# Attention and a multiplicative feed-forward on one core: the first two score groups of each batch change places, and the order of all work is recomputed

## The chip, the cores and the metric

The kernel runs on one core of a Trainium2 chip. The core has TensorE (PE, matrix products), ScalarE (ACT), VectorE (DVE), GpSimd (POOL) and SyncE (SP). DMAs are issued by POOL, SP and, once, ACT. The metric is the time of one execution on the device in microseconds (us); of several runs the median is taken.

## The reference

There are 8 batches and 8 heads, 576 queries and keys of 64 numbers per head, and 16 beacon keys and values per head, which every query sees. The other keys are causal.

```python
k_all = np.concatenate([beacon_k, k], axis=2)          # 16 + 576 keys
v_all = np.concatenate([beacon_v, v], axis=2)
scores = scale * np.matmul(q, k_all.transpose(0, 1, 3, 2))
causal[:, Nb:] = np.triu(np.ones((S, S), dtype=bool), k=1)
scores = np.where(causal, -1e9, scores)
a = np.exp(scores - scores.max(-1, keepdims=True))
a /= a.sum(-1, keepdims=True) + 1e-09
attn = np.matmul(a, v_all)                             # then x = tokens x (heads * 64)
a = x @ w1; b = x @ w2
h = a * b @ w3
return (h @ w_out).astype(np.float32)                  # 4608 x 512
```

w1 and w2 are 512 x 1024, w3 is 1024 x 1024 and w_out 1024 x 512.

## The kernel before

The program is one long list, ORDER, of small steps separated by semicolons. It was computed ahead of time. A step is a name with numbers: `s 0 1 2` is the function s with batch 0, group 1, bank 2. The loop at the end calls them one after the other, and each engine runs its own instructions in exactly this order. An instruction waits until the data that it reads is there and the place that it writes is free; everything behind it on its engine waits with it.

**Loads.** lq, lk and lv load chunks of queries, keys and values (128 tokens, all heads; of batch 0 a chunk number of lq and lk is a pair of heads instead), lkb and lvb the beacon keys and values, l1 and l2 quarters of w1 and w2, l3 eighths of w3, lo quarters of w_out. All but the first two (S and A) are issued by POOL, which also issues most stores (st); at most eight of its DMAs are under way in the trace at a time.

**Queries and keys.** In batch 0, cast turns a pair of heads into 16-bit numbers (ACT or DVE), tq or tk transposes it on TensorE, eq or ek copies it out. In batch 1 and for part of batch 2 there is no cast. Other chunks are transposed by a DMA that SP issues (Dq, Dk). tn and en do the same for the beacon keys of batch 0.

**Scores.** A batch is four pairs of heads (t) with 13 groups of blocks. A group fills 512 columns of each head's scores. make_groups lists them: for each t a corner group (the blocks with the first 112 queries, which see the beacon, and those with the last 80), and runs of four 128 x 128 blocks that NINE lists. s computes a group in two banks, exp evicts it on ACT to one of eight ring slots (line 517), m masks the diagonal blocks (DVE, line 527), v multiplies by the values (line 538), n divides by the sums (DVE, lines 549 and 550).

**Between.** x (TensorE, line 564) and ex, or TX (a DMA of SP), transpose the result to xT.

**Feed-forward.** W = w3 @ w_out is formed once: t3 transposes an eighth of w3, e3 copies it out, f multiplies by w_out (line 492), ew copies the result out. For each of nine blocks of 512 tokens (mc), a and b are the products with w1 and w2 (line 579), ea scales and copies a (ACT or DVE, lines 299 and 301), eb multiplies it by b (DVE, line 594), o multiplies by W (line 600), eo copies out, st stores.

**Banks.** The last number of a step on TensorE is its bank: 0 is a pair for scores, 6 and 7 are single ones, 2 with 3 and 4 with 5 are used as a pair or as two. A step waits until the copy that reads its bank's last content is done.

**Spins.** spin multiplies zeros, to keep TensorE at work before there is data.

Of the kernel before, what the change touches and what calls it, by code (L numbers as in the profile page):

```python
# [696 lines left out]
```

## Time and profile before

| | us |
|---|---|
| median of 4 runs (291.25 to 292.49) | 291.94 |
| the profiled execution's own time | 292.93 |
| its span, first to last instruction | 291.2 |
| TensorE busy | 283.9 |
| DVE, ACT, POOL busy | 171.7, 147.3, 134.3 |

The profile is of one execution. A busy share in it is an average over a head in which data arrives, a long middle and an end. A TensorE step's duration overlaps the next one's; the time from one start to the next is what it costs. The clock granted to TensorE has a mean of 0.998.

### The profile page before, as it was taken

How to read it: one execution, taken by the hardware profiler on the slowest of the kernel's cores; microseconds unless marked ns; L12 is line 12 of the kernel's file. 1: busy time of each engine (PE TensorE's matmuls, PEld its weight loads, DVE VectorE, ACT ScalarE, POOL GpSimd, SP SyncE). 2: the span in 40 equal slices, each digit the busy share in tenths (PEclk: the TensorE clock that was granted, in tenths of full speed). 3: DMA queues.
4: the chain of work that ended last, by engine and by line, in shares of the span. 5: the costliest groups of instructions: out<-in, count | busy, mean ns of one | idle time of the engine just before them, and what ended most of it. 6: DMA issues, size and time to landing. Idle time of an engine off the chain costs nothing.

```text
span 291.2 us, 7032 instructions
## 1 busy us (share of the span) xinstructions
PE 283.9 (97%) x2904; PEld 153.9 (53%) x2904; DVE 171.7 (59%) x370; ACT 147.3 (51%) x188; POOL 134.3 (46%) x187
## 2 busy tenths in 40 slices
PE   7999999999999999999999999999999999999993
PEld 3536675565565555565544555555555445444442
DVE  4344587885686847565562666565755575677600
ACT  3767779636574655588126567547482162000031
POOL 8869888797569551384098554630010011000000
PEclk9999999999999999999999999999999999999999
DMA  9999999999999999699999999996220015100043
GB/s 163 199 200 174 172 174 177 170 154 140 162 203 144 131 157 211 114 130 169 150 137 129 202 205 155 150 193 140 47 92 2 36 66 143 55 2 0 23 157 110
DMA packets 154319, 38.87 MB, mean 133 GB/s; under 512 B 144112, under 2 KB 150000, under 8 KB 154288
## 3 DMA queue, kind: packets, MB, share of 16 engines
q0 software_dynamic: 114800, 26.46, 107.1%
q1 hardware_dynamic: 39280, 11.68, 26.7%
q8 instruction: 23, 0.38, 0.5%
q10 hardware_dynamic: 208, 0.29, 0.4%
q14 instruction: 8, 0.07, 0.1%
HBM read 39.32 MB, written 9.44 MB: 167 GB/s over the span
## 4 chain that ended last, share of the span: by engine, by line
PE 75%; DMA 14%; POOL 8%; issue 1%; ACT 0%; POOLq 0%; SPq 0%
PE one L579 38%; PE one L600 21%; PE one L538 8%; PE pair L507 7%; DMA w<-in_moe_w_dram 5%; DMA st<-in_k_dram 2%; DMA qT<-q 2%; POOL va L339 2%; DMA wo<-in_moe_w_out_dram 2%; POOL q L331 2%; DMA q<-in_q_dram 2%; POOL k L339 1%; POOL w L389 1%; POOL xT L398 1%; PE one L564 0%
## 5 line engine op out<-in xcount | busy, mean ns | idle before, releaser
L579 PE MATMUL one<-xT,w 128*128 128x512 f16 x576 | 133.6, 379 | 0.0
L517 ACT ACTIVATE ring<-pair 128x1024 f16<-128x1024 f32 x104 | 99.2, 1027 | 21.4 <-PE pair L507 19.4
L579 PEld LDWEIGHTS <-w 128*128 128x128 f16 x576 | 52.9, 98 | 59.4 <-issue 2.5
L600 PE MATMUL one<-Wt,gT 128*128 128x512 f16 (+1 forms) x296 | 66.5, 374 | 0.0
L594 DVE TENSOR_TENSOR gT<-one,asb 128x512 f16<-128x512 f32 x72 | 49.1, 689 | 23.2 <-PE one L579 16.3
L299 ACT ACTIVATE asb<-one 128x512 f32<-128x512 f32 x32 | 19.2, 600 | 75.4 <-PE one L579 49.4
L614 POOL DMA_DIRECT2D out_dram<-st x27 | 15.3, 569 | 63.3 <-DVE st L301 29.5
L600 PEld LDWEIGHTS <-gT 128*128 128x128 f16 x296 | 27.7, 98 | 30.7 <-issue 1.3
L339 POOL DMA_DIRECT2D va<-in_v_dram x40 | 34.0, 853 | 20.7 <-PE one L538 15.4
L538 PEld LDWEIGHTS <-ring 128*128 128x128 f16 x960 | 35.2, 97 | 9.9 <-issue 1.0
L538 PE MATMUL one<-va,ring 128*128 128x65 f16 x960 | 37.6, 193 | 0.0
L301 DVE TENSOR_SCALAR asb<-one 128x512 f32<-128x512 f32 x40 | 27.5, 689 | 14.8 <-PE one L579 14.0
L339 POOL DMA_DIRECT2D k<-in_k_dram x35 | 29.8, 857 | 13.3 <-DMA kT<-k 9.4
L331 POOL DMA_DIRECT2D q<-in_q_dram x35 | 30.0, 863 | 7.7 <-DMA va<-in_v_dram 2.6
L550 DVE TENSOR_TENSOR x<-one,rd 128x384 f16<-128x384 f32 (+1 forms) x64 | 31.4, 491 | 2.2
L507 PE MATMUL pair<-qT,kT 64*128 64x80 f16 (+4 forms) x736 | 30.8, 225 | 0.1
L507 PEld LDWEIGHTS <-kT 64*128 64x128 f16 x736 | 19.8, 95 | 14.7 <-issue 11.9
L299 ACT ACTIVATE st<-one 128x512 f32<-128x512 f32 (+1 forms) x18 | 10.3, 574 | 24.3 <-PE one L600 24.0
L527 DVE TENSOR_TENSOR ring<-ring,MD 128x768 f16<-128x768 f16 x32 | 17.7, 552 | 7.9 <-ACT ring L517 7.9
L301 DVE TENSOR_SCALAR st<-one 128x512 f32<-128x512 f32 x19 | 13.1, 690 | 14.1 <-PE one L600 14.1
L527 DVE TENSOR_TENSOR ring<-ring,MX 128x384 f16<-128x384 f16 x32 | 11.3, 354 | 16.4 <-ACT ring L517 16.4
L549 DVE RECIPROCAL rd<-one 128x6 f32<-128x6 f32 (+1 forms) x64 | 11.7, 183 | 12.2 <-PE one L538 11.9
(63 smaller groups left out, 134.8 us busy)
## 6 DMA issues: line engine op xcount, KB each, us to landing
out_dram<-st POOLq DMA_DIRECT2D x27, 256.0 KB, 7.3
q<-in_q_dram POOLq DMA_DIRECT2D x28, 128.0 KB, 6.8
va<-in_v_dram POOLq DMA_DIRECT2D x24, 128.0 KB, 7.4
k<-in_k_dram POOLq DMA_DIRECT2D x21, 128.0 KB, 7.1
xT<-in_moe_w_dram POOLq DMA_DIRECT2D x8, 256.0 KB, 6.2
w<-in_moe_w_dram POOLq DMA_DIRECT2D x8, 256.0 KB, 7.3
out_dram<-st SPq DMA_DIRECT2D x8, 256.0 KB, 2.0
wo<-in_moe_w_out_dram POOLq DMA_DIRECT2D x4, 256.0 KB, 6.2
```

Source lines behind the costliest of these rows:

```text
L299: nc.scalar.activation(dst, src, AF.Copy, scale=by)
L301: nc.vector.tensor_scalar(dst, src, by, None, ALU.mult)
L331: nc.gpsimd.dma_start(dst[:rows, c], src[b, :, ds(c * P, rows), :].rearrange("h s d -> s h d"))
L339: nc.gpsimd.dma_start(dst[ds(p0, rows), c], src[b, :, ds(s0, rows), :].rearrange("h s d -> s h d"))
L507: nc.tensor.matmul(shape(n, "pair")[:, hh, ds(col, w)], kT[ds(hh * 64, 64), t, ts(jt, P)], qT[ds(hh * 64, 64), t, ds(q0, w)],)
L517: nc.scalar.activation(held(b, g)[:, :, 0:GW], shape(n, "pair"), AF.Exp, scale=scale)
L527: nc.vector.tensor_tensor(blk, blk, msk, ALU.mult)
L538: nc.tensor.matmul(pv[:, 2 * at + hh, 0 : D + 1], held(b, g)[:, hh, ds(col, P)], va[:, jt, 2 * t + hh, 0 : D + 1], start=(jt == 0), stop=( ...
L550: nc.vector.tensor_tensor(x16s[b % NB2][:, ds(2 * h, ni), ts(t, P)].rearrange("p i (h d) -> p i h d", h=2), pv[:, 0 : 2 * ni, 0:D].rearran ...
L579: nc.tensor.matmul(bank(n), w12[:, kt, ds(i * DF + kf * P, P)], xT[:, kt, ds(mc * 512, 512)], start=(kt == 0), stop=(kt == NKT - 1),)
L594: nc.vector.tensor_tensor(gTs[mc % 2][:, kf, :], bank(n), asb[slot["asb", (mc, kf)]], ALU.mult)
L600: nc.tensor.matmul(bank(n)[:, 0:w], gTs[mc % 2][:, kf, ts(mt, P)], Wt[:, kf, ds(c0, w)], start=(kf == 0), stop=(kf == NFT - 1),)
```

## The change

make_groups appends the corner group of the first pair of heads behind the first run instead of ahead of it. So group 0 of each batch now holds the blocks of keys 1, 3, 2 and 2 (in chunks of 128) with queries 112 to 495, none of which reads chunk 0, where the beacon keys lie; group 1 is the corner. Other groups keep their numbers. All of ORDER is new: the sequence of steps, their banks, which engine copies, which chunks of x go by TensorE and which by DMA, and the order of the loads. The steps are the same ones but for these choices, one spin entry less (20 spins become 17) and the split of the last o, eo and st (256 and 256 columns become 384 and 128).

```diff
     for t in range(4):
         corner = [(t, 0, 0, 0, 112), (t, 4, 4, 112, 80)]
         corner += [(t, j, 4, 192 + 80 * j, 80) for j in range(4)]
-        groups.append(corner)
+        if t:
+            groups.append(corner)
         for jt, i in NINE[t]:
             run.append((t, jt, i, 128 * len(run), 128))
             if len(run) == 4:
                 groups.append(run)
                 run = []
+                if len(groups) == 1:
+                    groups.append(corner)
```

The head of ORDER up to the first scores of batch 1, the places where batch 2 begins, and the end:

```diff
-consts 0; lq 0 0 S; lk 0 0 A; l3 6; consts 1; spin 8 7; lq 1 2 P; l3 4; lo 1; lkb 0 P;
-cast 0 0 q A; lo 0; cast 0 0 k D; lkb 1; consts 2; spin 2 7; tq 0 0 6; tk 0 0 7; eq 0 0 D 6;
-lq 0 1 P; ek 0 0 A 7; spin 1 0; t3 6 5; lk 0 1 P; e3 6 A 5; spin 1 6; tq 1 2 6; l3 3; eq 1 2 A 6;
-spin 3 7; t3 4 7; lvb 0; e3 4 D 7; lo 2; spin 3 6; tn 0 6; en 0 A 6; lk 1 0 P; spin 1 7; s 0 0 0;
-s 0 1 2; s 0 2 4; exp 0 0 0; f 6 0 7; l3 0; f 4 0 6; lk 0 2 P; exp 0 2 4; m 0 0 0; f 6 1 7;
-cast 0 1 q D; lo 3; f 4 1 6; cast 0 1 k D; exp 0 1 2; tq 0 1 5; lk 0 3 P; tk 0 1 4; ek 0 1 D 4;
-eq 0 1 A 5; spin 1 0; t3 3 3; lq 0 3 P; m 0 0 1; l3 5; s 0 3 0; s 0 4 4; e3 3 D 3; exp 0 3 0;
-f 6 2 7; lvb 1; f 3 0 3; exp 0 4 4; m 0 1 0; l3 2; s 0 5 0; tk 1 0 2; f 3 1 3; exp 0 5 0; t3 0 5;
-lq 0 2 P; f 3 2 3; e3 0 D 5; ek 1 0 A 2; lk 1 1 P; f 4 2 6; cast 0 2 k A; m 0 1 1; f 0 0 4;
-f 0 1 4; lv 0 4; f 0 2 4; f 6 3 7; cast 0 3 k A; l3 1; f 0 3 4; ew 6 D 7; lv 0 0; tk 0 3 5;
-ew 0 A 4; f 4 3 6; cast 0 3 q D; ek 0 3 A 5; tq 0 3 7; ew 4 D 6; t3 5 4; lv 1 0; eq 0 3 A 7;
-f 3 3 3; e3 5 D 4; lv 0 2; tk 0 2 6; ew 3 A 3; t3 2 7; ek 0 2 A 6; lv 0 3; f 5 0 5; e3 2 D 7;
-f 5 1 5; cast 0 2 q A; lv 0 1; f 5 2 5; f 5 3 5; lq 1 3 P; tq 0 2 6; ew 5 D 5; tk 1 1 7;
-eq 0 2 A 6; f 2 0 4; l1 2; ek 1 1 D 7; s 0 6 0; s 0 7 2; l3 7; exp 0 6 0; t3 1 6; lq 1 1 P;
-f 2 1 4; e3 1 D 6; f 2 2 4; exp 0 7 2; lq 1 4 P; f 2 3 4; m 0 2 0; lq 1 0 P; f 1 0 7; ew 2 A 4;
-f 1 1 7; lk 1 2 P; f 1 2 7; f 1 3 7; lk 1 3 P; v 0 1 0 6; ew 1 A 7; v 0 2 0 5; n 0 1 0 6; tq 1 3 4;
-lk 1 4 P; v 0 0 0 7; n 0 2 0 5; eq 1 3 A 4; s 0 8 0; n 0 0 0 7; v 0 0 1 6; exp 0 8 0; lv 1 3;
-s 0 9 2; s 0 10 4; s 0 11 0; n 0 0 1 6; exp 0 9 2; l1 0; t3 7 7; m 0 2 1; v 0 1 1 6; e3 7 D 7;
-exp 0 11 0; lv 1 1; tq 1 1 3; tq 1 4 2; n 0 1 1 6; f 7 0 7; eq 1 4 A 2; l2 0; f 7 1 7; exp 0 10 4;
-m 0 3 0; s 0 12 0; m 0 3 1; lq 2 1 P; v 0 3 0 6; eq 1 1 D 3; tk 1 2 2; exp 0 12 0; v 0 2 1 5; l1 1;
-n 0 3 0 6; f 7 2 7; n 0 2 1 5; ek 1 2 A 2; lv 1 2; x 0 4 6; x 0 0 4; v 0 3 1 3; ex 0 4 A 6;
-ex 0 0 D 4; l2 1; f 7 3 7; n 0 3 1 3; tq 1 0 6; lv 1 4; tk 1 4 5; tk 1 3 4; eq 1 0 D 6; ek 1 4 A 5;
-x 0 2 3; x 0 3 2; lq 2 0 P; ek 1 3 D 4; ex 0 2 A 3; x 0 1 6; ex 0 3 D 2; s 1 0 0; s 1 1 4; s 1 2 2;
...
-Dk 2 3; v 1 3 0 3; exp 1 12 4; ea 0 5 D 7; b 0 6 2; lq 3 2 P; ek 2 4 D 6; m 1 3 1; b 0 4 6; lv 2 2;
-n 1 3 0 3; v 1 3 1 7; eb 0 6 2; x 1 4 5; x 1 0 4; n 1 3 1 7; lq 3 4 P; tk 2 1 3; b 0 5 2;
-ek 2 1 A 3; ex 1 0 D 4; lk 3 2 P; ex 1 4 D 5; v 1 2 1 7; eb 0 5 2; Dq 2 4; tq 2 2 5; lk 3 1 P;
-b 0 7 4; n 1 2 1 7; eq 2 2 A 5; lk 3 4 P; a 0 4 5; eb 0 7 4; lvb 2; Dq 3 1; x 1 1 7; ea 0 4 A 5;
-lq 3 3 P; x 1 3 4; ex 1 1 D 7; x 1 2 3; tq 2 3 2; ex 1 3 A 4; eb 0 4 6; o 0 2 7; ex 1 2 A 3;
-lk 4 3 P; eq 2 3 D 2; Dq 3 2; lq 3 0 P; eo 0 2 D 7; s 2 0 0; s 2 1 4; s 2 2 2; exp 2 0 0; lk 4 0 P;
...
-o 7 3 7; eo 7 2 D 6; st 7 2 S; o 7 0 6; eo 7 3 A 7; st 7 3 S; o 8 3 7; eo 7 0 A 6; st 7 0 S;
-o 7 1 6; eo 8 3 A 7; st 8 3 S; o 8 2 7; eo 7 1 A 6; st 7 1 S; o 8 0 6 0 256; eo 8 2 A 7; st 8 2 S;
-eo 8 0 A 6 0 256; st 8 0 S 0 256; o 8 0 5 256 256; eo 8 0 A 5 256 256; st 8 0 S 256 256
+consts 0; lq 0 0 S; lk 0 0 A; l3 5; consts 1; spin 8 7; lkb 0 P; lk 0 2 P; lq 0 1 P; l3 2; lo 0;
+cast 0 0 q D; l3 0; consts 2; cast 0 0 k D; spin 1 7; tq 0 0 6; lv 0 2; eq 0 0 D 6; tk 0 0 7;
+ek 0 0 A 7; spin 1 0; t3 5 5; l3 3; s 0 0 0; lk 0 1 P; e3 5 D 5; tn 0 6; cast 0 2 k A; lo 1;
+en 0 D 6; spin 2 7; s 0 1 2; s 0 2 4; cast 0 1 q A; lk 1 1 P; tk 0 2 6; exp 0 2 4; tq 0 1 7; lo 3;
+eq 0 1 D 7; ek 0 2 A 6; t3 2 5; f 5 0 7; lo 2; exp 0 1 2; e3 2 D 5; spin 1 6; f 2 0 6; exp 0 0 0;
+m 0 0 0; lv 0 1; t3 0 5; lkb 1; e3 0 A 5; m 0 0 1; f 0 0 4; l3 4; t3 3 5; cast 0 1 k A; lq 0 2 P;
+e3 3 D 5; spin 3 0; tk 0 1 3; f 3 0 5; lq 1 2 P; ek 0 1 D 3; f 5 1 7; f 3 1 5; lv 0 3; spin 1 3;
+tk 1 1 3; f 2 1 6; ek 1 1 A 3; f 0 1 4; l3 6; s 0 3 0; s 0 4 2; exp 0 3 0; f 3 2 5; lk 1 0 P;
+f 3 3 5; exp 0 4 2; m 0 1 0; lv 0 4; s 0 5 0; ew 3 D 5; f 0 2 4; l3 1; exp 0 5 0; f 0 3 4; f 5 2 7;
+lvb 0; ew 0 A 4; t3 4 5; m 0 1 1; lv 0 0; f 5 3 7; cast 0 2 q A; e3 4 D 5; f 2 2 6; lq 0 3 P;
+tq 1 2 4; ew 5 D 7; f 4 0 5; f 4 1 5; eq 1 2 D 4; lk 0 3 P; f 4 2 5; f 4 3 5; t3 6 7; l2 1;
+ew 4 A 5; tq 0 2 4; e3 6 D 7; tk 1 0 3; lk 1 2 P; eq 0 2 A 4; f 2 3 6; ek 1 0 D 3; ew 2 A 6;
+s 0 6 0; s 0 7 4; l3 7; f 6 0 7; exp 0 6 0; lkb 2; t3 1 6; f 6 1 7; lv 1 0; exp 0 7 4; m 0 2 0;
+v 0 0 1 3; lk 1 4 P; cast 0 3 q D; s 0 8 0; e3 1 A 6; n 0 0 1 3; lq 1 1 P; tq 0 3 5; v 0 1 0 4;
+v 0 2 0 2; eq 0 3 D 5; exp 0 8 0; lq 1 3 P; v 0 0 0 6; n 0 2 0 2; f 1 0 3; lv 1 2; cast 0 3 k A;
+f 1 1 3; n 0 0 0 6; f 1 2 3; lq 1 0 P; n 0 1 0 4; tk 1 2 6; tk 0 3 5; ek 1 2 A 6; f 6 2 7; m 0 2 1;
+f 6 3 7; ek 0 3 A 5; lvb 1; lq 1 4 P; ew 6 D 7; s 0 9 0; s 0 10 4; l1 3; exp 0 9 0; t3 7 6;
+tk 1 4 7; lk 1 3 P; v 0 1 1 2; e3 7 D 6; exp 0 10 4; f 1 3 3; m 0 3 0; l1 0; tq 1 1 6; ek 1 4 D 7;
+ew 1 A 3; s 0 11 0; s 0 12 4; n 0 1 1 2; l1 2; tq 1 3 7; exp 0 11 0; v 0 3 0 3; eq 1 1 D 6; l2 0;
+v 0 2 1 2; eq 1 3 D 7; exp 0 12 4; m 0 3 1; tq 1 0 6; lv 1 3; f 7 0 7; eq 1 0 D 6; f 7 1 7;
+lq 2 0 P; n 0 2 1 2; tq 1 4 6; v 0 3 1 5; eq 1 4 A 6; n 0 3 0 3; f 7 2 7; l1 1; f 7 3 7; n 0 3 1 5;
+lq 2 2 P; x 0 0 6; ew 7 A 7; x 0 4 4; tk 1 3 3; ex 0 0 D 6; x 0 3 5; lv 1 4; ex 0 4 A 4;
+ek 1 3 D 3; x 0 1 7; x 0 2 6; ex 0 3 A 5; ex 0 1 D 7; lv 1 1; s 1 0 0; s 1 1 2; s 1 2 4;
...
+tq 2 0 5; ea 0 3 D 7; a 0 2 6; lq 2 3 P; eq 2 0 A 5; m 1 1 1; v 1 1 0 7; lv 2 0; v 1 0 1 4;
+ea 0 2 A 6; n 1 1 0 7; tq 2 2 5; b 0 3 6; n 1 0 1 4; lvb 2; eq 2 2 A 5; v 1 0 0 7; lk 2 4 P;
+eb 0 3 6; s 1 6 0; s 1 7 2; s 1 8 4; Dk 2 0; n 1 0 0 7; exp 1 6 0; a 0 7 6; lq 2 1 P; exp 1 8 4;
+m 1 2 0; b 0 4 7; lk 2 3 P; exp 1 7 2; m 1 2 1; tk 2 2 5; lv 2 4; v 1 2 0 4; ek 2 2 D 5; lkb 3;
+s 1 9 0; s 1 10 2; Dq 2 4; n 1 2 0 4; exp 1 9 0; v 1 1 1 5; lq 3 2 P; eb 0 4 7; a 0 6 4;
+exp 1 10 2; m 1 3 0; ea 0 7 D 6; tq 2 3 7; lv 2 1; s 1 11 0; s 1 12 2; ea 0 6 A 4; eq 2 3 D 7;
+v 1 3 0 6; lk 3 0 P; n 1 1 1 5; Dq 3 4; exp 1 11 0; v 1 2 1 7; n 1 3 0 6; tk 2 4 4; lkb 4; a 0 5 5;
+exp 1 12 2; lk 2 1 P; ek 2 4 D 4; m 1 3 1; x 1 0 6; x 1 4 4; tq 2 1 3; lv 2 2; ex 1 0 D 6;
+ex 1 4 A 4; v 1 3 1 2; eq 2 1 D 3; Dk 2 3; b 0 6 6; n 1 2 1 7; lv 2 3; b 0 2 4; n 1 3 1 2;
+lq 4 1 P; eb 0 6 6; x 1 2 7; lq 3 0 P; x 1 1 3; Dq 3 2; ex 1 2 A 7; x 1 3 2; eb 0 2 4; b 0 7 6;
+lk 3 2 P; ex 1 3 A 2; ex 1 1 D 3; b 0 5 7; ea 0 5 D 5; lv 3 0; Dk 3 0; eb 0 7 6; b 1 2 4; lk 3 3 P;
+eb 0 5 7; o 0 3 6; lk 3 1 P; a 1 2 7; lk 4 4 P; eo 0 3 D 6; tk 2 1 5; ea 1 2 D 7; a 1 3 6;
+ek 2 1 A 5; lk 3 4 P; eb 1 2 4; s 2 0 0; s 2 1 2; s 2 2 4; ea 1 3 A 6; exp 2 1 2; b 1 0 7; lvb 3;
...
+a 7 5 4; eb 8 6 6; o 8 1 7; eb 7 3 5; ea 7 5 D 4; eb 7 5 3; o 7 3 6; eo 8 1 D 7; st 8 1 S; o 7 1 7;
+eo 7 3 A 6; st 7 3 S; o 8 0 6; eo 7 1 A 7; st 7 1 S; o 7 2 7; eo 8 0 D 6; st 8 0 S; o 8 3 6;
+eo 7 2 A 7; st 7 2 S; o 7 0 7; eo 8 3 A 6; st 8 3 S; o 8 2 6 0 384; eo 7 0 D 7; st 7 0 S;
+eo 8 2 A 6 0 384; st 8 2 S 0 384; o 8 2 5 384 128; eo 8 2 D 5 384 128; st 8 2 S 384 128
```

## The prediction

> **What bounds the kernel now.** I read the page's first two parts, then TensorE by stretches, its waits, the chain, and last the loads one by one.
>
> ```profile
> PE 283.9 (97%) x2904; PEld 153.9 (53%) x2904; DVE 171.7 (59%) x370; ACT 147.3 (51%) x188; POOL 134.3 (46%) x187
> PE   7999999999999999999999999999999999999993
> POOL 8869888797569551384098554630010011000000
> DMA  9999999999999999699999999996220015100043
> ```
>
> TensorE is busy for 97% of the span; ACT and DVE have room. POOL, which issues the loads, and the DMA engines are full for the first third. By stretches:
>
> ```profile
> 0.00:20.00 20.00, 18.12 (x155) 9.06 (x156) 8.51 (x25) 11.83 (x15) 15.10 (x31) 1.00 1.15 185
> 20.00:40.00 20.00, 19.20 (x274) 12.37 (x273) 11.57 (x28) 14.70 (x21) 18.59 (x24) 1.00 1.94 175
> 40.00:60.00 20.00, 20.00 (x288) 12.12 (x285) 15.66 (x37) 15.76 (x20) 16.36 (x22) 1.00 2.03 174
> 60.00:80.00 20.00, 19.93 (x238) 11.42 (x237) 12.91 (x31) 10.32 (x14) 15.50 (x20) 1.00 2.24 151
> 80.00:240.00 160.00, 160.00 (x1704) 86.60 (x1703) 99.18 (x215) 87.36 (x108) 67.71 (x91) 1.00 1.46 134
> ```
>
> Columns: stretch, its length, then the busy time of PE, weight loads, DVE, ACT, POOL; clock, DMA share, GB/s. TensorE loses time before 40 us and none from 80 to 240. So the order decides two things: how late TensorE runs behind its loads in the head, and whether some later transfer misses it. The chain says the same:
>
> ```profile
> 47.33 7.94 DMA w<-in_moe_w_dram
> 55.55 0.86 POOL q L331
> 56.41 5.17 DMA q<-in_q_dram
> 61.65 6.99 DMA qT<-q
> 68.69 0.79 PE pair L507 x20
> ...
> 245.23 27.63 PE one L579 x128
> 272.86 13.85 PE one L600 x72
> ```
>
> Up to 68.69 us the end is traced back through loads, behind it through TensorE alone. Two rows give the price of TensorE's steps:
>
> ```profile
> 160.66 0.86 PE one L579 x4
> 161.53 0.77 PE pair L507 x22
> 162.30 0.97 PE one L579 x4
> ```
>
> Four products of L579 take 0.86 us, and 0.97 beside scores: going from a score matmul (64 rows) to another kind, or back, costs 0.10. From start to start I read per step: a, b 0.862; o 1.726; f 0.431; v 0.367 and 0.543; a score group 0.224; t3 0.458; a transposed chunk 0.22 to 0.26; a spin 0.215, each of the first eight 0.423.
>
> **The change part by part.** *The swap itself.* All score groups, products and score matmuls (736) remain. Of 104 groups 63 follow another group directly in both orders, so there are 82 changes of kind at 0.10 in both: nothing. In batch 0 the first group can start before the beacon's transpose: its scores move from 10.64 us to about 7.2, but nothing behind them starts earlier than its own load.
>
> *Spins.* 20 become 17: 3 x 0.215 = 0.6 us less TensorE work. It is a gain only if TensorE isn't waiting for a load there instead.
>
> *Evictions and transposes.* ACT and DVE swap a few copies (ea 32 to 31 on ACT, eq 8 to 4); 17 x steps and 23 TX remain, three of each changing places. Covered by engines at 51% and 59%; uncovered, one is 0.6 to 1.0 us. SP has 76 transposes before and after; their order changes, its first comes earlier (below).
>
> *The loads' order, the term that counts.* Landing times are issue plus time to landing, by tile. In the head POOL's loads land one behind the other, at intervals that depend on the kind: 256 KB of weights 1.25 us, a batch-0 pair of heads 0.73, a 128 KB chunk 0.87, 112 KB 0.76, 80 KB 0.52, 64 KB 0.45, a beacon 0.2. From the first landing at 6.26 these intervals give l3 0 at 17.53 (17.47 in the trace). Then one load (lk 0 2, issued 12.08) lands at 19.33 instead of 18.2, and all later ones run 0.6 to 0.9 late.
>
> The last load that stops TensorE for certain in the old head is lq 1 4, landing at 36.56, the 35th on POOL; its transposes start at 36.61. Summing the steps behind that point: 241.6 + 70 changes x 0.097 = 248.4. The trace has its last matmul done at 286.69, that is 250.1: 1.65 of small rests, which I carry over.
>
> In the new order the corresponding load is lq 1 0, the 38th. Ahead of it stand the same loads but for: lv 1 2 (0.87), lk 1 2 (0.87), lk 1 4 (0.52) and lq 1 0 in place of lq 1 4 (0.42): 36.56 + 2.68 = 39.24. The start adds some: the old stream began with two weights and a chunk in its first three loads, a backlog; the new one has the beacon and two pairs behind one weight, and none of the head's loads landed sooner than 4.8 us after its issue. By that bound the third and fourth (issued about 2.9 and 3.5) land at 7.7 and 8.3 instead of 7.2 and 7.9: 0.4 to 0.7. So lq 1 0 lands at 39.6 to 39.9; I take 39.75. Behind tq 1 0 stand 240.1 + 66 x 0.097 = 246.5 us of TensorE work. End of TensorE: 39.75 + 0.05 + 246.5 + 1.65 = 288.0, against 286.7: **+1.3**.
>
> As a check from the other side, what TensorE waits for on its way. tq 0 1 waits for lq 0 1 (8.3 to 8.6) and its cast, now on ACT (0.83 instead of 0.36 to 0.41 on DVE): 0.5. t3 2 waits for bank 5, pair 4 being read by an exp (1.02): 0.65. f 0 0 follows t3 0 at once and waits for e3 0, now on ACT behind two exps (1.01 instead of 0.69): 1.3; behind it on TensorE stands t3 3, whose weights land at 14.1 to 14.5 anyway. tk 0 1 waits for another cast on ACT: 0.5. tk 1 1 waits for lk 1 1: 0.4. f 3 2 needs lo 2, now the last of its four (about 20.5; the old order had lo 2 at 15.45 and lo 3 at 20.26): 0.8. With 0.7 ahead of the first transpose and some 1.6 of smaller ones: 6.5, against 4.9 in the same reckoning of the old order. 1.7 less 0.6 of spins is +1.1. I take +1.2.
>
> *Later stages.* Scores of batches 2 to 7 start by TensorE's own sum 2.0, 0.9, 1.5, 5.0, 0.1 and 14.7 us later than before, besides the lag; their last key or query load stands 3.2, 1.0, 3.0, 2.8, 1.9 and 5.1 us of intervals later. Slack of the old trace covers most (Dk 3 3 lands at 90.2 for scores at 92; the last of batch 4 at 114.9 for 118). Two places have almost none: lv 1 1 for v 1 1 (about 52) and lk 2 1 for s 2 0 (about 72.3). I add 0.1, with bounds 0 and 1.5.
>
> *End.* The last piece is 128 columns wide, not 256: its copy is at most the 0.38 of the old one, its transfer at most the old 3.2. I take -0.1; bounds -0.4 and 0.
>
> Sum: 1.2 + 0.1 - 0.1 = +1.2. The span goes from 291.2 to 292.4; the profiled execution's own time of 292.93 (1.7 around the span) becomes 294.1. It lay 1.0 above the median of four runs, 291.94, to which the same +1.2 gives **293.1**.
>
> **One rule against the rows.** The clock. In the trace the first eight spins take 0.423 and later ones 0.215: TensorE comes up at half rate. The new head has fewer spins and a longest wait of 1.3 us. If the clock fell back once, and took as long to return, 8 x 0.208 = +1.7 us would be lost.
> The Trainium skill, "TensorE: Matmul & The Clock Gate" (Part 1), has the clock fall only after an idle window of about 3.4 us; by it, estimated, 1.3 us of waiting costs no clock and the sum stays at +1.2. No run yet shows such a gap.
>
> **The rivals.**
> *Not slower: the stream keeps its intervals.* The lag at lk 0 2 belongs to one moment, not to every order. Without it lq 1 0 lands at 38.9 or sooner, and f 3 2 waits 0.1 instead of 0.8: about +0.3, 292.2. For it: l3 0 and everything ahead of it land within 0.1 of the intervals. Against: most loads up to 50 us stay late. It decides if lq 1 0 lands before 38.9. If the start bound falls too (0.5) and TensorE has only the old head's 4.3 us of waits, its work allows 33.7 + 4.3 = 38.0 at tq 1 0: -0.5 or, with some evictions earlier, 290.8; that is the faster side.
> *Slower by more: batch 2 misses its keys.* SP's first transpose goes out at about 54 instead of 57.25, and four, not three, go out ahead of lk 2 1. In the old trace loads fell behind their intervals by 1.1 us after three transposes and 2.3 after four. lk 2 1, at 66.9 by intervals, lands at 69.3 and is transposed on TensorE at 71.1. It decides if the four cost over 4 us: then s 2 0 and all behind it wait, +1.5 on top, 294.6.
> *The clock falls back once:* 294.8, as above.
>
> **How the numbers follow.** Forecast 0.50 (own range 292.4 to 293.9; 0.12 of it under 292.8); stream undisturbed 0.25 (0.20 within, 0.05 below); batch 2 late 0.15; clock 0.05; faster through earlier evictions 0.05. A measurement here can tell about 0.3%, 0.9 us. Faster 0.05 + 0.05 = 0.10; within 0.20 + 0.12 = 0.32; slower 0.38 + 0.15 + 0.05 = 0.58. Range: 291.3 (the 38.0 above) to 295.2 (both slow rivals' part, or a later miss).
>
> **What would show it.** Right: TensorE busy for under 18 us in the first 20; f 0 0 and f 3 2 starting about 1 us late; tq 1 0 at 39.8; no idle time from 80 to 240; 17 spins. Wrong: tq 1 0 before 38.9, matmuls of 0.42 after 10 us, or a wait at s 2 0. What I may have wrong above all is the landing intervals in a new order.

## The result, and the profile after

The changed kernel takes 292.68 us (median of 54 runs, 291.34 to 296.45). The kernel before, run beside it, takes 292.04 us (78 runs, 291.18 to 294.21). The ratio is 1.0022 with a 95% interval of 1.0013 to 1.0031: slower, by 0.64 us. (One of the 54 executions, that of 296.45 us, was in a slower state and is left out of the ratio.) That is inside the range on record (291.3 to 295.2) and has the sign that was forecast, but it is half of the +1.2 us, and by the bound of 0.3% it counts as "within", which had been given a chance of 0.32 against 0.58 for "slower".

The profiled execution of the changed kernel has a span of 290.7 us and an own time of 292.38 us. The span of the one before was 291.2 us, although its kernel is the faster one. The reason lies behind TensorE's last matmul. In the old execution 4.5 us followed it, because its last store took 3.2 us to land; in other executions with the same end, shown below, that store lands in 1.7 us and about 3.1 us follow. In the changed one 3.1 us follow. So the two are compared by TensorE's end: 286.69 us before, 287.56 us after, +0.87.

The page of the changed kernel, its first two parts:

```profile
PE 283.2 (97%) x2901; PEld 154.2 (53%) x2901; DVE 171.7 (59%) x372; ACT 146.7 (50%) x186; POOL 134.7 (46%) x187
...
PE   6989999999999999999999999999999999999995
...
POOL 8868996999537783402985400577020001000000
...
DMA  7999999999999999995999991499983012300033
```

As before, TensorE is busy for 97%, and the only slices that are not full lie in the head and at the end. By stretches (stretch, length, busy time of PE, weight loads, DVE, ACT, POOL; clock, DMA share, GB/s):

```profile
0.00:20.00 20.00, 15.94 (x125) 8.23 (x125) 8.74 (x24) 9.03 (x11) 15.35 (x29) 1.00 1.17 180
20.00:40.00 20.00, 19.83 (x294) 12.80 (x293) 12.12 (x30) 15.60 (x21) 17.83 (x26) 1.00 1.85 177
40.00:60.00 20.00, 19.86 (x270) 11.94 (x270) 14.42 (x35) 14.56 (x20) 16.94 (x23) 1.00 2.09 167
60.00:80.00 20.00, 20.00 (x213) 11.19 (x213) 14.01 (x32) 10.57 (x16) 16.44 (x21) 1.00 2.40 166
80.00:240.00 160.00, 160.00 (x1724) 87.08 (x1723) 99.00 (x213) 86.84 (x107) 67.08 (x90) 1.00 1.39 135
```

TensorE was busy for 18.12 us of the first 20 before and is busy for 15.94 now; from 20 to 40 us it gains 0.63, from 40 to 60 it loses 0.14. From 60 to 240 us it never stops. So whatever the change costs is decided before 60 us. The chain of work that ended last, up to 55 us and its two longest pieces at the end (start, length, what):

```profile
11.20 9.16 DMA wo<-in_moe_w_out_dram
...
22.50 6.28 DMA xT<-in_moe_w_dram
...
41.70 8.32 DMA w<-in_moe_w_dram
50.06 1.04 PE one L583 x4
...
246.96 26.76 PE one L583 x124
273.72 13.85 PE one L604 x72
```

Before, the chain ran through loads up to 68.69 us. Now the last load on it is l1 1, a quarter of w1, which lands at 50.02 us (41.70 + 8.32), and from 50.06 TensorE alone sets the end. The loads ahead of it are lo 2 (landing at 20.37) and l3 1 (28.78), one behind the other in POOL's queue: none of them is a load of queries.

To see how much TensorE waited, I took the distance from each of its steps to the next and subtracted the step's own length from the prediction (and 0.10 for a change between scores and other work). What is left, summed in us:

| start of the step | 0 to 20 | 20 to 40 | 40 to 60 | 60 to 100 | behind 100 | sum |
|---|---|---|---|---|---|---|
| before | 2.49 | 1.81 | 0.32 | 0.43 | 0.69 | 5.74 |
| after | 5.55 | 0.31 | 0.63 | 0.12 | 0.59 | 7.20 |

That is 1.46 more, and three spins less are 0.64 of work less: +0.82, close to the +0.87 of TensorE's end. The waits moved to the first 20 us, where the 5.55 also hold about 1 us of a slow start of this execution (last section). The prediction had named the others; TensorE's own list of waits and its order of time show the longest:

```profile
PE one L496 <- ACT gT L299: 1.1, 1, 1.1
PE one L425 <- DVE o16q L299: 1.0, 1, 1.0
PE one L487 <- ACT ring L521: 0.5, 1, 0.5
```

L496 is f 0 0 behind e3 0 on ACT, L425 the first transpose, L487 is t3 2 behind an exp.

### The profile page after: what moved, and what is told of

It is laid out like the page before. It is cut to its first block, busy times and chain, and to the rows that moved or that the text cites. A ratio compares the mean times of both kernels' runs of the same rounds, so it can differ in the third digit from the quotient of the medians.

```text
span 290.7 us, 7027 instructions
## 1 busy us (share of the span) xinstructions
PE 283.2 (97%) x2901; PEld 154.2 (53%) x2901; DVE 171.7 (59%) x372; ACT 146.7 (50%) x186; POOL 134.7 (46%) x187
## 4 chain that ended last, share of the span: by engine, by line
PE 82%; DMA 8%; POOL 8%; issue 1%; DVE 0%; POOLq 0%
PE one L583 42%; PE one L604 22%; PE one L542 9%; PE pair L511 8%; DMA wo<-in_moe_w_out_dram 3%; DMA w<-in_moe_w_dram 3%; DMA xT<-in_moe_w_dram 2%; POOL va L343 1%; POOL q L335 1%; POOL k L343 1%; POOL w L393 1%; PE one L568 1%; POOL xT L402 1%; POOL st L360 1%; POOL wo L405 1%
## 5 line engine op out<-in xcount | busy, mean ns | idle before, releaser
L604 PE MATMUL one<-Wt,gT 128*128 128x512 f16 (+2 forms) x296 | 66.5, 373 | 0.0
L618 POOL DMA_DIRECT2D out_dram<-st x27 | 15.3, 565 | 83.5 <-ACT st L303 22.8
L303 ACT ACTIVATE asb<-one 128x512 f32<-128x512 f32 x31 | 18.5, 599 | 57.9 <-PE one L583 42.8
L542 PEld LDWEIGHTS <-ring 128*128 128x128 f16 x960 | 34.6, 97 | 9.0 <-issue 1.1
L303 ACT ACTIVATE st<-one 128x512 f32<-128x512 f32 (+1 forms) x19 | 11.3, 595 | 36.5 <-PE one L604 36.5
L305 DVE TENSOR_SCALAR st<-one 128x512 f32<-128x512 f32 (+1 forms) x18 | 12.0, 669 | 25.4 <-PE one L604 25.4
```

Of the source, the lines that this page charges most:

```text
L303: nc.scalar.activation(dst, src, AF.Copy, scale=by)
L305: nc.vector.tensor_scalar(dst, src, by, None, ALU.mult)
L542: nc.tensor.matmul(pv[:, 2 * at + hh, 0 : D + 1], held(b, g)[:, hh, ds(col, P)], va[:, jt, 2 * t + hh, 0 : D + 1], start=(jt == 0), stop=( ...
L604: nc.tensor.matmul(bank(n)[:, 0:w], gTs[mc % 2][:, kf, ts(mt, P)], Wt[:, kf, ds(c0, w)], start=(kf == 0), stop=(kf == NFT - 1),)
```

## The experiments

Five theories were put to the chip. **A**: the order of the loads sets the pace; TensorE comes to the same places at the same times whatever it loses ahead of them. **B**: in the profiled execution TensorE's rate rose late (half rate until 10 us), and that is the cost. **C**: the copies that moved to ACT (the casts of pair 1, e3 0) are the cost. **D**: the swap of the groups itself costs. **E**: the new split of the last block, 384 and 128 columns, costs or gains.

All ratios are to the kernel before, run on the same chip in the same job.

| run | ratio, 95% interval | median us | TensorE's end us |
|---|---|---|---|
| after | 1.0022, 1.0013 to 1.0031 | 292.68 | 287.56 |
| e1: two spins more | 1.0013, 0.9992 to 1.0033 | 292.70 | 287.24 |
| e2: three copies on DVE | 1.0041, 1.0018 to 1.0063 | 293.16 | 288.24 |
| e3: five loads later | 1.0001, 0.9984 to 1.0019 | 292.12 | 287.27 |
| e7: corner group first | 1.0024, 1.0003 to 1.0045 | 292.88 | 287.00 |
| e9: one weight earlier | 1.0064, 1.0046 to 1.0081 | 293.71 | 288.06 |
| e10: the old end | 1.0029, 1.0009 to 1.0049 | 292.66 | 287.78 |
| e12: e1, e3 and e10 | 1.0003, 0.9983 to 1.0023 | 292.04 | 286.88 |
| e5: before with 17 spins | 1.0002, 0.9985 to 1.0019 | 291.70 | 286.50 |
| e8: before with loads later | 0.9967, 0.9947 to 0.9986 | 290.97 | 285.98 |
| e13: e8 and e5 | 0.9966, 0.9945 to 0.9987 | 291.17 | 286.33 |
| e6: before with the new end | 1.0037, 1.0022 to 1.0051 | 292.99 | 286.91 |
| e11: e6 again | 1.0033, 1.0019 to 1.0047 | 292.72 | 287.13 |

TensorE's end is that of the one profiled execution. It scatters: after, e1, e2, e7 and e10, whose ratios do not differ beyond their intervals, lie between 287.0 and 288.2. The ratios carry the verdicts; the profiles tell where. A ratio of one of these runs is known to about 0.2%, 0.6 us.

### e1: two spins more ahead of the first transpose

```diff
-cast 0 0 q D; l3 0; consts 2; cast 0 0 k D; spin 1 7; tq 0 0 6; ...
+cast 0 0 q D; l3 0; consts 2; cast 0 0 k D; spin 3 7; tq 0 0 6; ...
```

> The changed kernel with two more spins (3 for 1) ahead of the first transpose, so that TensorE has no idle microsecond before its first data. In the changed kernel's trace spins and transposes up to about 10 us cost twice what they cost later (a spin 0.42, t3 5 0.99 against 0.45). Theory A (the loads set the pace: TensorE catches up with its loads at tq 1 0 and tq 1 4, near 40 us, and time saved before is only spent waiting there): the first 20 us look better, the time changes by less than 0.3 us. Theory B (the late rise of TensorE's rate is what the change costs): t3 5 takes 0.45 and the time falls by 0.6 to 1.3 us.

Measured: 1.0013 (0.9992 to 1.0033), the same as the changed kernel within the intervals. In its profile the rate is up from the fifth microsecond on, and TensorE is a whole microsecond ahead at 14 us. TensorE in order of time, the changed kernel first (start, length, engine, line, operation; in brackets the idle time before and what ended it):

```profile
7.76 1.06 PE L487 MATMUL one<-ident,xT 128*128 128x128 f16 x8
...
15.64 0.61 PE L496 MATMUL one<-wo,gT 128*128 128x512 f16 x2 [1.10 <-ACT gT L299]
...
30.14 0.71 PE L542 MATMUL one<-va,ring 128*128 128x65 f16 x18
```

and e1:

```profile
6.78 0.61 PE L487 MATMUL one<-ident,xT 128*128 128x128 f16 x8
...
14.58 0.60 PE L496 MATMUL one<-wo,gT 128*128 128x512 f16 x2 [1.10 <-ACT gT L299]
```

The eight products of the first line take 1.06 us at half rate and 0.61 at full rate, and f 0 0 starts at 15.64 or at 14.58. At v 0 0 1 nothing of it is left: 30.14 in the changed kernel, 30.16 in e1. The lead went into waits for what loads bring: 0.40 at tk 0 1 (its cast), 0.43 at f 3 2, which started at 20.47 with lo 2 landing at 20.43, and 0.14 at v 0 0 1, at 30.16 with lv 0 0 landing at 30.03. So B is not what this execution shows, and A has its first support: a microsecond gained in the first 15 is given back by 30. The ratio alone would not settle it, since B's smallest gain (0.6 us, a ratio of 1.0001) lies inside the interval.

### e2: three copies back on DVE

```diff
-... cast 0 1 q A; lk 1 1 P; ...
+... cast 0 1 q D; lk 1 1 P; ...
-m 0 0 0; lv 0 1; t3 0 5; lkb 1; e3 0 A 5; m 0 0 1; f 0 0 4; l3 4; t3 3 5; cast 0 1 k A; lq 0 2 P;
+m 0 0 0; lv 0 1; t3 0 5; lkb 1; e3 0 D 5; m 0 0 1; f 0 0 4; l3 4; t3 3 5; cast 0 1 k D; lq 0 2 P;
```

> The changed kernel with three copies of the head moved from ACT to DVE: cast 0 1 of q and of k, and e3 0, behind which f 0 0 waits 1.1 us. Theory A (loads set the pace): f 0 0 starts about 0.3 us earlier and less is waited there, but tq 1 4 still starts at about 40.8 and the time changes by less than 0.3 us. Theory C (waits behind copies on ACT add to the end): 0.5 to 1.2 us less.

Measured: 1.0041 (1.0018 to 1.0063). The wait did shrink, as TensorE's order of time shows:

```profile
15.22 0.60 PE L496 MATMUL one<-wo,gT 128*128 128x512 f16 x2 [0.79 <-DVE gT L299]
```

0.79 us idle instead of 1.10, and f 0 0 starts 0.42 us sooner (0.1 of it because this execution came to it sooner). v 0 0 1 starts at 30.21, no sooner than in the changed kernel (30.14), and the median is no better. C falls: the longest wait that the prediction named is real, and worth nothing.

### e3: five loads moved behind the last one that the head needs

In the changed kernel l2 1, lkb 2, lv 1 0, lv 1 2 and lvb 1 stand among the loads that land from 32 to 40 us. Here they stand behind l2 0.

```diff
-... f 4 3 5; t3 6 7; l2 1;
+... f 4 3 5; t3 6 7;
-... exp 0 6 0; lkb 2; t3 1 6; f 6 1 7; lv 1 0; ...
+... exp 0 6 0; t3 1 6; f 6 1 7; ...
-... n 0 2 0 2; f 1 0 3; lv 1 2; cast 0 3 k A;
+... n 0 2 0 2; f 1 0 3; cast 0 3 k A;
-f 6 3 7; ek 0 3 A 5; lvb 1; lq 1 4 P; ...
+f 6 3 7; ek 0 3 A 5; lq 1 4 P; ...
-... eq 1 1 D 6; l2 0;
+... eq 1 1 D 6; l2 0; l2 1; lkb 2; lv 1 0; lv 1 2; lvb 1;
```

> The changed kernel with five loads that are not needed until 52 us (l2 1, lkb 2, lv 1 0, lv 1 2, lvb 1; 3.3 us of landing intervals) moved behind l2 0, so that lq 1 0, lq 1 4 and lk 1 3 land about 3 us earlier. Theory A (loads set the pace): TensorE no longer waits at tq 1 4, where it lost 0.25 us; the next load that holds it is lq 0 3 at about 31, so the time falls by 0.2 to 0.4 us and not by 3. Theories B and C (the head's rate or its copies): no change, 0.1 at most.

Measured: 1.0001 (0.9984 to 1.0019), median 292.12: level with the kernel before. The interval just touches that of the changed kernel (0.9984 to 1.0019 and 1.0013 to 1.0031), so that the gain of 0.2% is likely rather than certain from this run alone; e12 below gives the same ratio. How it comes is not how I had it. TensorE in order of time, the changed kernel first:

```profile
38.60 1.08 PE L542 MATMUL one<-va,ring 128*128 128x65 f16 x30
39.51 0.38 PE L431 MATMUL one<-ident,q 128*128 128x128 f16 x4
...
40.84 0.29 PE L431 MATMUL one<-ident,q 64*128 64x64 f16 x4
```

and e3:

```profile
31.20 0.43 PE L425 MATMUL one<-ident,o16q 96*128 96x96 f16 x6 [0.22 <-DVE o16q L299]
...
38.69 1.07 PE L542 MATMUL one<-va,ring 128*128 128x65 f16 x30
39.60 0.39 PE L431 MATMUL one<-ident,q 128*128 128x128 f16 x4
```

L431 at 39.51 is tq 1 0, the step at which the prediction put the end of the waits. In the changed kernel its load lands at 39.41, in e3 at 36.49, three microseconds earlier, and tq 1 0 starts at 39.60. In both it follows the v ahead of it by 0.91 us. So lq 1 0 did not hold TensorE, which arrived at 39.5 for other reasons: in the changed kernel's execution its slow start, in e3 the loads that land ahead of 31 us and that e3 does not move (0.36 us beyond the step's pace at f 3 2 for lo 2, and the cast behind lq 0 3, whose 0.22 us stand in the first line). What e3 takes away are two waits behind tq 1 0: 0.15 us at tq 1 4 for lq 1 4 (landing at 40.80 in the changed kernel, 37.02 here) and 0.23 at a 0 3 for l1 1 (50.02, and 49.31 here). That is 0.38 of the 0.6 us; the rest can't be read from one execution of each. The wait for l1 1 is not there in every execution: it is 0.23 us in the profile of the changed kernel, 0.43 in e2, 0.51 in e10, 0.09 in e7 and nothing in e1; in e3 and e12, which move the loads, there is none. The times have the same shape: the fastest quarter of the changed kernel's executions ends at 292.22 us and its slowest begins at 293.15, those of e3 at 292.00 and 292.25, so that most of the gain lies in the longer executions. The stretch from 40 to 60 us in e3:

```profile
40.00:60.00 20.00, 20.00 (x278) 12.36 (x276) 14.88 (x37) 14.91 (x21) 17.16 (x22) 1.00 2.13 169
```

20.00 us busy where the changed kernel has 19.86.

### e9: one quarter of w2 moved ahead of an eighth of w3

The opposite of e3, as a test of A with the sign turned round: l2 1 goes ahead of l3 4.

```diff
-m 0 0 0; lv 0 1; t3 0 5; lkb 1; e3 0 A 5; m 0 0 1; f 0 0 4; l3 4; t3 3 5; ...
+m 0 0 0; lv 0 1; t3 0 5; lkb 1; e3 0 A 5; m 0 0 1; f 0 0 4; l2 1; l3 4; t3 3 5; ...
-... f 4 3 5; t3 6 7; l2 1;
+... f 4 3 5; t3 6 7;
```

> The changed kernel with one load of 256 KB (l2 1, needed at 53 us) moved forward on POOL's queue, ahead of l3 4, so that the fourteen loads between its two places land one interval, 1.25 us, later and those behind unchanged. Theory A: t3 4 and tq 0 3 start about 1.0 us later and nothing gives it back, the time rises by 0.8 to 1.2 us against the changed kernel (1.0 to 1.8 us against before). Theories B, C and D (rate, copies, swap): no change.

Measured: 1.0064 (1.0046 to 1.0081), 0.42% or 1.2 us above the changed kernel. The weight loads of TensorE in order of time, and then its products:

```profile
23.75 0.45 PEld L487 LDWEIGHTS <-xT 128*128 128x128 f16 x8 [1.31 <-DMA xT<-in_moe_w_dram]
```

```profile
31.99 0.43 PE L425 MATMUL one<-ident,o16q 96*128 96x96 f16 x6
...
40.40 0.38 PE L431 MATMUL one<-ident,q 128*128 128x128 f16 x4
```

l3 4 lands at 23.71 instead of 22.56 and t3 4 waits for it; 0.98 us of that is more than the order's own pace. The line at 31.99 (tq 0 3) stood at 31.11 in the changed kernel, tq 1 0 at 39.51. lq 1 0 lands at 39.24 here, even a little sooner, and TensorE is 0.9 us later all the same. One 256 KB load that goes ahead of the wrong one costs the kernel about its own interval, 1.25 us in the prediction's reckoning. A stands, and the load that counts is once more not lq 1 0. The execution of e9 had come to t3 4 sooner than the changed kernel's (22.8 us, had it not waited, against 23.41), and it lost nothing at a 0 3, so the ends of the two profiles lie only 0.5 us apart. (The edit delays twelve loads, not the fourteen of the expectation.)

### e7: the corner group first again

Everything of the new order is kept, but batch 0's group with the beacon keys goes first, as in the old one.

```diff
-ek 0 0 A 7; spin 1 0; t3 5 5; l3 3; s 0 0 0; lk 0 1 P; e3 5 D 5; tn 0 6; cast 0 2 k A; lo 1;
-en 0 D 6; spin 2 7; s 0 1 2; s 0 2 4; ...
+ek 0 0 A 7; spin 1 0; t3 5 5; l3 3; tn 0 6; en 0 D 6; s 0 1 0; lk 0 1 P; e3 5 D 5; cast 0 2 k A; lo 1;
+spin 2 7; s 0 0 2; s 0 2 4; ...
-... exp 0 1 2; e3 2 D 5; spin 1 6; f 2 0 6; exp 0 0 0;
+... exp 0 0 2; e3 2 D 5; spin 1 6; f 2 0 6; exp 0 1 0;
```

> The changed kernel with the swap undone in batch 0 alone: the corner group of the first pair of heads is again the first to be computed, behind the beacon's transpose; the loads and all else stay. Theory A (the loads' order is what costs, the swap itself nothing): the first scores start about 0.5 us later, the time changes by less than 0.3 us. Theory D (the swap itself is what moves the time): a change of 0.5 us or more, in either direction.

Measured: 1.0024 (1.0003 to 1.0045), the changed kernel's own ratio. The group of four full blocks starts at 9.50 us instead of 8.76 (the corner group, now the first, at 8.11), and v 0 0 1 starts at 29.81, not later. Nothing speaks for D: neither the swap nor the earlier start that it allows is worth anything that shows here, though the interval leaves room for 0.2% either way. The profile of this run holds a surprise, told in the last section.

### e10: the old end on the changed kernel

```diff
-... o 8 2 6 0 384; ... eo 8 2 A 6 0 384; st 8 2 S 0 384; o 8 2 5 384 128; eo 8 2 D 5 384 128; st 8 2 S 384 128
+... o 8 2 6 0 256; ... eo 8 2 A 6 0 256; st 8 2 S 0 256; o 8 2 5 256 256; eo 8 2 A 5 256 256; st 8 2 S 256 256
```

> The changed kernel with the old end: last product, copy and store split 256 and 256 columns, last copy on ACT. The old kernel with the new end was 0.37% slower than before, against what was expected. Theory E (the 384 and 128 split is itself what makes the changed kernel slower, by some 0.6 to 1.0 us): 0.6 to 1.0 us less than the changed kernel, level with before. Theory A (the loads' order): no change beyond 0.2 us, 0.1 to 0.3% above before; the time from TensorE's last matmul to the end stays at 3.1.

Measured: 1.0029 (1.0009 to 1.0049), median 292.66 against 292.68. The end is worth nothing in the changed kernel; E falls for it. The run also shows again the wait that the prediction had not seen. TensorE in order of time:

```profile
50.29 1.04 PE L583 MATMUL one<-xT,w 128*128 128x512 f16 x4 [0.34 <-DMA w<-in_moe_w_dram]
```

a 0 3 waits for l1 1, which landed at 50.24 in this execution, 0.5 us beyond its pace.

### e6 and e11: the new end on the kernel before

```diff
-... o 8 0 6 0 256; ... eo 8 0 A 6 0 256; st 8 0 S 0 256; o 8 0 5 256 256; eo 8 0 A 5 256 256; st 8 0 S 256 256
+... o 8 0 6 0 384; ... eo 8 0 A 6 0 384; st 8 0 S 0 384; o 8 0 5 384 128; eo 8 0 D 5 384 128; st 8 0 S 384 128
```

> The kernel before with the changed kernel's end: the last product, copy and store split into 384 and 128 columns instead of 256 and 256, the last copy on DVE. In the two traces the time from the last matmul's end to the end of the span was 4.55 us before and 3.12 after. If the split makes that difference: 1.0 to 1.4 us less. If the 4.55 was one late DMA of that execution and the split brings only its shorter copy: 0.1 to 0.3 us less, and the profile shows about 3.1 us.

> The kernel before with the changed kernel's end, once more, as six runs are few. Theory E: again 0.3% or more slower than before, with over 3.5 us from the last matmul to the end. Theory A: within 0.2% of before, about 3.1 us.

Measured: 1.0037 (1.0022 to 1.0051), and again, on another chip, 1.0033 (1.0019 to 1.0047): a third of a per cent slower, though the last copy is shorter. The last copy of e6, in order of time (0.38 us in the old order):

```profile
286.95 0.29 DVE L301 TENSOR_SCALAR st<-one 128x128 f32<-128x128 f32 x1 [9.69 <-PE one L600]
```

and how long the last stores take to land, first of the old kernel's profile, whose end is the old one:

```profile
DMA to landing us min/median/max: 1.7/2.4/3.2
```

of e5, which has the same end:

```profile
DMA to landing us min/median/max: 1.7/1.7/1.7
```

of e6:

```profile
DMA to landing us min/median/max: 1.9/2.0/2.4
```

and of the changed kernel:

```profile
DMA to landing us min/median/max: 1.7/1.9/2.0
```

The last store, 128 columns wide, lands 2.43 us after its issue in e6 and in e11 alike, against 1.7 us for the 256 columns of e5. That is 0.7 of the 1 us that this end costs there. In the changed kernel the same narrow store lands in 1.7 to 1.8 us. Why it takes longer in the one order than in the other isn't settled, and no run was made for it. The 3.2 us of the old kernel in the first fence are one late store of one execution: e5, with the same end, has none.

### e12: e1, e3 and the old end together

The loads stand as in e3, the end as in e10, and the spins as in e1:

```diff
-cast 0 0 q D; l3 0; consts 2; cast 0 0 k D; spin 1 7; ...
+cast 0 0 q D; l3 0; consts 2; cast 0 0 k D; spin 3 7; ...
-... eq 1 1 D 6; l2 0;
+... eq 1 1 D 6; l2 0; l2 1; lkb 2; lv 1 0; lv 1 2; lvb 1;
-eo 8 2 A 6 0 384; st 8 2 S 0 384; o 8 2 5 384 128; eo 8 2 D 5 384 128; st 8 2 S 384 128
+eo 8 2 A 6 0 256; st 8 2 S 0 256; o 8 2 5 256 256; eo 8 2 A 5 256 256; st 8 2 S 256 256
...
```

> The changed kernel with three edits together: two more spins ahead of the first transpose, the five early loads moved back behind l2 0, and the old end. Theory A: the loads' edit alone counts; as with it alone, level with before, 0.4 to 0.8 us under the changed kernel. Theory E: a further 0.6 to 1.0 us less, 0.2 to 0.3% faster than before.

Measured: 1.0003 (0.9983 to 1.0023), median 292.04. It repeats e3's result, and adding spins and the old end to the load edit adds nothing that shows. l1 1 lands at 49.19 and no step waits for it.

### e5: the kernel before without three spins

```diff
-spin 3 7; t3 4 7; lvb 0; e3 4 D 7; lo 2; spin 3 6; tn 0 6; en 0 A 6; ...
+spin 3 7; t3 4 7; lvb 0; e3 4 D 7; lo 2; tn 0 6; en 0 A 6; ...
```

> The kernel before with 17 spins instead of 20 (the three ahead of tn left out). This is the term of 0.6 us in the prediction. Theory A (TensorE waits for its loads there in any case): tn waits for lkb 0 instead, the time changes by less than 0.2 us. The prediction's term: 0.6 us less. Theory B (spins keep TensorE's rate up): steps behind 10 us take up to twice as long, 0.5 us more or worse.

Measured: 1.0002 (0.9985 to 1.0019). The beacon's transpose behind those spins waited 0.20 us for its load and now waits 0.90: the 0.6 us of spins stood where TensorE would have waited. The term "three spins less, -0.6" is worth nothing.

### e8 and e13: the kernel before with loads moved back

If loads set the pace in the old order too, moving those back that nothing needs yet must make it faster. Six loads move (the expectations say seven).

```diff
-spin 3 7; t3 4 7; lvb 0; e3 4 D 7; ...
+spin 3 7; t3 4 7; e3 4 D 7; ...
-f 6 2 7; lvb 1; f 3 0 3; ...
+f 6 2 7; f 3 0 3; ...
-f 0 1 4; lv 0 4; f 0 2 4; ...
+f 0 1 4; lv 0 4; lvb 0; f 0 2 4; ...
-... t3 5 4; lv 1 0; eq 0 3 A 7;
+... t3 5 4; eq 0 3 A 7;
-eq 0 2 A 6; f 2 0 4; l1 2; ek 1 1 D 7; ...
+eq 0 2 A 6; f 2 0 4; ek 1 1 D 7; ...
-... eq 1 4 A 2; l2 0; f 7 1 7; exp 0 10 4;
+... eq 1 4 A 2; l2 0; lv 1 0; lvb 1; f 7 1 7; exp 0 10 4;
-... tq 1 0 6; lv 1 4; tk 1 4 5; ...
+... tq 1 0 6; lv 1 4; l1 2; tk 1 4 5; ...
...
```

Further on, lv 2 0 and lv 2 3 go behind lq 2 4 in the same way. e13 takes the three spins out as well.

> The kernel before with seven loads that have 15 us or more to spare moved back on POOL's queue (lvb 0, lvb 1, lv 1 0, l1 2 in the head; lv 2 0 and lv 2 3 behind lq 2 4), nothing else changed. Theory A (the loads set the pace in this kernel too): the waits of TensorE between 20 and 40 us fall from 1.8 to about 1.0, the wait at s 2 0 goes, the time falls by 0.5 to 0.9 us. Otherwise (TensorE or copies set it): no change.

> The kernel before with the seven loads moved back and with 17 spins, that is, the two edits together that gave 0.33% and nothing when made alone. Theory A (the loads set the pace, spins stand where TensorE waits in any case): as with the loads alone, 0.2 to 0.45% faster than before. If the spins' 0.6 us comes free once the loads hold TensorE less: 0.5% or more faster.

Measured: e8 0.9967 (0.9947 to 0.9986), median 290.97; e13 0.9966 (0.9945 to 0.9987). **This is faster than both kernels**, than the old one by about 1 us, and the spins again add nothing. TensorE of the old kernel around tk 0 3, and at the two transposes in a row of which the second is tq 1 4, in order of time:

```profile
17.98 3.35 PE L492 MATMUL one<-wo,gT 128*128 128x512 f16 x14
21.96 0.43 PE L421 MATMUL one<-ident,o16k 96*128 96x96 f16 x6 [0.64 <-ACT o16k L295]
...
36.28 0.61 PE L427 MATMUL one<-ident,q 128*128 128x128 f16 x8
```

and of e8, at the same places:

```profile
18.36 3.28 PE L492 MATMUL one<-wo,gT 128*128 128x512 f16 x14
21.59 0.43 PE L421 MATMUL one<-ident,o16k 96*128 96x96 f16 x6
...
35.59 0.60 PE L427 MATMUL one<-ident,q 128*128 128x128 f16 x8
```

e8 came to the f's 0.38 us later than the old kernel (18.36 against 17.98; its first microseconds went worse) and left them 0.37 us sooner, because lk 0 3 lands at 20.62, not 21.00, and tk 0 3 waits 0.11 us beyond its pace for the cast, not 0.80. The transposes of the last line start at 35.59, in the old kernel at 36.28; the rest of that lead comes from t3 2 (l3 2 lands at 23.85, not 24.35) and tq 1 3 (lq 1 3 at 31.56, not 32.63). lq 1 4 has no part in it: it lands at 34.20 here, at 36.56 in the old kernel, and tq 1 4 follows tq 1 3 by 0.32 us here and by 0.33 there. The stretch of e8 from 20 to 40 us:

```profile
20.00:40.00 20.00, 19.93 (x295) 13.14 (x294) 12.03 (x29) 14.87 (x21) 18.56 (x24) 1.00 1.94 175
```

19.93 us busy against 19.20. The 0.7 us that e8 is ahead at 36 us is what it is ahead at the end: 285.98 against 286.69. A holds for both orders.

## Why the prediction was right or wrong

**What bounds the kernel: right.** The head decides, and behind 60 us TensorE never stops. The loads' order sets when TensorE is through the head: e3 takes the changed kernel's loss back with an edit of loads alone, e12 with the same edit (and spins and end, which moved nothing clear of the noise by themselves), e9 adds 1.2 us with one load, and e8 makes the old kernel 1 us faster.

**The swap itself, nothing: right as far as it was tested.** e7, 1.0024 against 1.0022, undoes it in batch 0 alone; in the other batches TensorE does not stop behind 60 us, with the new groups as with the old.

**Spins, -0.6: wrong, nothing.** e5. The prediction had said on what it depends (that TensorE isn't waiting there). The forecast's sum went by landings and did not contain this term; the check from the other side did.

**The waits named: two of six came in the profiled execution, and they are no costs.** f 0 0 waited 1.26 us (1.3 forecast), t3 2 0.66 (0.65). tq 0 1, tk 0 1, tk 1 1 and f 3 2, forecast at 2.2 us together, did not wait there. That the waits up to 40 us still sum to 5.9 us, 1.6 more than before, close to what was forecast, is luck: the slow start filled the place of those four. e2 cut the wait of f 0 0 and e1 gained a microsecond ahead of it, and neither came through: most of what TensorE gains in the first 15 us it loses by 31 us again, to tk 0 1 and f 3 2 above all. f 3 2, forecast to wait 0.8 us for lo 2, started at 20.80 with the load there since 20.37; in e1, e2, e3, e9 and e12, where TensorE came sooner or the load later, it waited, for 0.25 to 0.47. (In the forecast's list, 6.5 less 4.9 is 1.6, not 1.7.)

**The loads' order, the term that counts: the step that failed.** "In the new order the corresponding load is lq 1 0". The numbers around it came out: the third and fourth loads landed at 7.66 and 8.40 (7.7 and 8.3 forecast), lq 1 0 at 39.41 (39.75 taken, 39.6 to 39.9 the bounds), tq 1 0 started at 39.51 (39.8), and 248.05 us followed it (248.15). Yet e3 brought lq 1 0 three microseconds sooner and tq 1 0 stayed. Its counterpart had not held the old head either: "The last load that stops TensorE for certain in the old head is lq 1 4" rested on a landing at 36.56 and a start at 36.61, but in e8 that load lands 2.4 us sooner and tq 1 4 still follows tq 1 3 at the same distance. Both loads landed just in time for a TensorE that came then for other reasons. So the step's good numbers are luck: the sum starts from a place where load and TensorE happened to meet, in both orders. What holds TensorE in the new order, where its first 15 us go well, are loads landing from 15 to 31 us (lk 0 1, lo 2, lq 0 3, and l3 4 in e9), and then, by 0.15 and 0.23 us in the changed kernel's profile, lq 1 4 and l1 1. In that profile none of the earlier ones held it: f 3 2 came 0.43 us behind its load and t3 4 0.85. How much each of them is worth stays open, as no run brought one of them forward.

**Its size.** The term was 1.3, taken as 1.2 with the check. TensorE's end moved by 0.87 in the two profiles, and the median by 0.64. Of the difference to the profiles, 0.29 is the start of tq 1 0 (39.51 for 39.80) and 0.10 what followed it (248.05 for 248.15). That, and what the median has less than the profiles, lies within what TensorE's end scatters from one execution to the next.

**Later stages, +0.1: near it in sum (-0.1), not in place.** lk 2 1 landed at 67.89, not 69.3, and s 2 0 started at 72.33 (72.3 forecast) without a wait. Behind 60 us the waits shrank by 0.41 us in sum. But from 40 to 60 they grew by 0.31, for lq 1 4 and l1 1, of which the prediction says nothing.

**End, -0.1: nothing** (e10).

**The rivals.** "The stream keeps its intervals" was to decide itself at lq 1 0 before 38.9; it landed at 39.41. Its time, 292.2, is nonetheless about as near to 292.68 as the forecast's 293.1, since its other half, f 3 2 hardly waiting, did come in the profiled execution. "Batch 2 misses its keys" did not happen. "The clock falls back once" was priced at +1.7 us and given 0.05. It did happen in one profiled execution, e7's, and cost nothing that shows at the end; the last section shows it. The price had counted what TensorE loses there and not what the loads give back.

## What to carry to other kernels

Where TensorE is full and loads land one behind the other in a fixed order, a wait or a slow stretch early in the head is free as long as a later load holds TensorE anyway; sum the loads ahead of each place where TensorE meets one, and look at the places with the least slack together, since the last of them need not be the one that sets the end. To find out which it is, move a load: bringing one sooner and seeing the step stay still (e3), or delaying one and seeing all that follows move (e9), told more than any row of waits. A load that lands just ahead of its step (lq 1 4 in the old order, lq 1 0 in the new one) need not hold it. Moving back the loads that are not needed yet was worth 1 us here in the old order, more than the whole recomputed order moved.
